# Spatial product and first output rows as half-array passes over two tiles at once, a second x group in two loads, and a newly searched order

## The chip, the cores and the metric

The kernel runs on one core of one Trainium2 chip. The core has five engines with an instruction queue each: TensorE (PE, matrix products), VectorE (DVE), ScalarE (ACT), GpSimd (POOL) and SyncE (SP, which here issues DMAs). Each queue is worked off strictly in its written order; between engines there are only semaphores. The metric is the device time of one execution in microseconds. Before the change it is 247.53 us, the median of 3 runs (247.49 to 248.48).

## The reference

Two layers on x with S = 2048 tokens and D = 448 features, all in bf16. LN is a layer norm without scale and shift.

```python
# A: windowed attention, 16 heads of 28, window of 8 keys, 2 apart, backwards
q, k, v = split(LN(x) @ wqkv)                   # wqkv 448 x 1344
attn = softmax(q . k[pos - 0, 2, ... 14] * 28 ** -0.5)
h = x + (attn @ v[same keys]) @ wo              # wo 448 x 448
# B: gated MLP with a product over tokens
z = gelu(LN(h) @ w_in)                          # w_in 448 x 1792
z1, z2 = z[:, :896], LN(z[:, 896:])
g = w_sp @ z2 + b_sp[:, None]                   # w_sp 2048 x 2048: mixes tokens
out = h + (z1 * g) @ w_out                      # w_out 896 x 448
```

Token t of g needs z2 of all 2048 tokens. So the spatial product (w_sp @ z2, the largest product of all) can begin a tile's sum with some tokens of z2, but can't end one before the last z2 tile is there.

## The kernel before, in words

Tokens are cut into 16 tiles of 128 (NB). Everything lies in SBUF; the regions of the attention stage are used again by weights and results of the gated MLP.

**Attention.** x comes in by loads of 1, 1, 2, 4, 4 and 4 tiles into `x_tm` (FIRST, `load_x`; loads have line 519 in the page, or 518 where they transpose). For each tile DVE makes the statistics (L610 BATCH_NORM_STATS2, L612 aggregate), POOL the reciprocal root for a whole group of tiles (`ln_rstd`, L604 and L605; the groups are LN1G), DVE the normalized `xn` (L621). The first four tiles are transposed on PE, the others by a transposing DMA on SP's queue (xT4 and up, into `xhT`). PE makes q and k (`qkT`), v (`V1`); small casts out of PSUM are shared between ACT and DVE (`move`, L504; the table ON says which one goes to another engine than its default). 18 blocks of queries follow: logits (L793) in small passes of 28 contraction rows, exp on ACT into `E` (L802), the mask on DVE (L808, `mk`), the product with V on PE (L817), division on DVE into `otm` (L828), a transposing DMA into `OT`, wo on PE, and the residual into x_tm on DVE (L760).

**Gated MLP.** Again statistics, root, norm, and a transposing DMA into `hnT`. Then 16 products z2_0 to z2_15 (a tile of 128 tokens, 2 x 448 columns) and 14 products z1_0 to z1_13 (2 x 512 columns, z1 transposed). ACT applies gelu; for those z2 tiles that are made while ACT still has exps to do, ACT first copies the raw sums out (z2c) and applies gelu later. DVE takes two statistics and an aggregate of each z2 tile (L877, L880), POOL makes the root for two tiles, DVE normalizes z2p in place (L886).

The spatial product has 28 tiles (fc, tc): 128 features fc by 512 tokens tc. Each is a sum over 16 token tiles s, written as four lots of 4 passes. Lot q of a tile needs the normalized z2 tiles 4q to 4q + 3:

```python
for q in range(4):
    ss = range(4 * q, 4 * q + 4)
```

A pass is one matmul instruction of the full array: 128 rows of contraction, 128 x 128 weights from `z2p`, 512 columns of `wsp_la`, `wsp_lb` or `wsp_hi`. DVE adds the bias (L957, `ub`) and multiplies into z1p (L962). After each seven tiles of one tc come four output tiles: 7 passes of 448 columns with `w_out` (L972), the residual on DVE (L979, `srg`), and the store.

**Half passes.** The contraction of a D = 448 product has three chunks of 128 and one of 64. `product()` (L461) writes the two sums of a ticket (a pair of PSUM banks) in one of three modes. FH and HF: six full passes and two half passes of 64 rows, or the other way round. AB: only half passes, two at a time. One half of the array works on the first sum with rows 0 to 63 of a chunk, the other half on the second sum with rows 64 to 127; then the halves change roles. Where one sum goes over from one half of the array to the other, the job is marked `own`, and PE waits on its own semaphore for the first half's last pass. Before the change the z products and nearly all others are in mode AB.

**The order.** Each job (a few instructions of one engine) stands in a list; a planner, run long before, has left two tables in the file: ORDER, the order in which the jobs are written into the queues, and BANKS, the PSUM banks of each ticket. Nothing is decided on the chip: an engine whose next instruction waits does no later one. `keys` and durations in the code were the planner's input, and no instruction comes out of them.

Of the kernel before, what the change touches and what calls it, by code (L numbers as in the profile page):

```python
# [6 lines left out]
D = 448  # L7
NHEAD = 16
DH = 28
FH = 896  # L10
EPS = 1e-5

NB = 16
# [16 lines left out]
ORDER = [0, 25, 27, 30, 28, 2, 938, 6, 31, 938, 938, 15, 938, 32, 938, 938, 128, 1, 938, 938, 39, 9, 26, 938, 41, 40,  # L30
# [169 lines left out]
class Ticket:  # L200
# [4 lines left out]
    def __init__(self, n):  # L205
        self.n = n
        self.b = None
        self.res = Res("ticket")


class Job:
    __slots__ = ("eng", "key", "dur", "lat", "ops", "acq", "rel", "tick",
                 "deps", "idx", "name", "tbl", "srv", "kind", "alts", "modes", "mate", "own")


class Planner:


    def __init__(self):
# [825 lines left out]
```

## Time and profile before

| | |
|---|---|
| median of 3 runs | 247.53 us |
| profiled execution | 246.68 us |
| its span | 245.0 us |
| mean granted TensorE clock | 1.000 |
| PE busy | 237.6 us (97%), 2139 instructions |
| DVE busy | 154.9 us (63%), 338 instructions |
| ACT busy | 92.6 us (38%) |
| POOL busy | 37.0 us (15%) |
| first spatial pass | 124.28 us from the span's start |
| PE's last pass ends by | 242.4 us |

The profiled execution is 1.68 us longer than its span and 0.85 us below the median. Busy shares are over the whole span: DVE's 63% is an average of a first half with nearly full slices and a second half in which it has little to do. Lines (L461) are those of the kernel before. Columns of a waits row are the total in us, the number of waits and the longest; of a group's row, busy time in us and the mean of one in ns, then the idle time ahead of them. In a timeline row stand the start, the length (for a run of several instructions, from the first's start to the last's end), the engine, the line and the instruction. PE's passes are pipelined, so lengths of single passes overlap; the step from one run's start to the next is the time that the passes took.

### The profile page before, as it was taken

The numbers are of one execution on the slowest core, as the hardware profiler recorded it, in microseconds if no ns is written. First come the engines' busy times: TensorE is split into PE (matmuls) and PEld (weight loads), VectorE is DVE, ScalarE is ACT, GpSimd is POOL, SyncE is SP. The second block draws the span as 40 slices with busy tenths as digits, with TensorE's granted clock in tenths as the row PEclk, the third lists the DMA queues.
The fourth block names the chain that finished last, engine by engine and source line by source line (L and its number), as shares of the span: only waits on it lengthen the run. The fifth ranks groups of instructions, "written<-read, shape, count | busy, mean of one in ns | idle before, by whom it ended". The sixth has DMA issues, their size and how long they took to land.

```text
span 245.0 us, 5076 instructions
## 1 busy us (share of the span) xinstructions
PE 237.6 (97%) x2139; PEld 119.9 (49%) x2139; DVE 154.9 (63%) x338; ACT 92.6 (38%) x111; POOL 37.0 (15%) x82
## 2 busy tenths in 40 slices
PE   7988999979999999999999999999999999999995
PEld 5764545444555544445444444444444444444453
DVE  5698989968997799899991120360333353271674
ACT  2379479775685979978740000000000000000000
POOL 6424020223042302323331000000000000000000
PEclk9999999999999999999999999999999999999999
DMA  5953656889969769988999400000000001001022
GB/s 144 268 171 67 89 89 118 150 182 150 219 92 162 119 94 201 238 134 119 197 195 176 98 0 0 3 0 0 0 3 0 1 19 56 3 30 45 0 65 87
DMA packets 66247, 23.16 MB, mean 95 GB/s; under 512 B 58672, under 2 KB 65968, under 8 KB 66224
## 3 DMA queue, kind: packets, MB, share of 16 engines
q1 hardware_dynamic: 66224, 22.83, 48.2%
q8 instruction: 17, 0.28, 0.5%
q14 instruction: 6, 0.05, 0.1%
HBM read 6.72 MB, written 1.84 MB: 35 GB/s over the span
## 4 chain that ended last, share of the span: by engine, by line
PE 84%; DVE 4%; DMA 4%; ACT 2%; SPq 2%; POOL 1%; issue 1%; DVEq 0%
PE psum L948 39%; PE psum L461 30%; PE psum L972 9%; PE psum L817 3%; DMA x_tm<-in_A_x_dram 2%; PE psum L793 2%; SPq L519 2%; DVE st L610 2%; DMA xhT<-xn 2%; ACT E L802 1%; DVE xn L621 1%; ACT qkT L504 1%; POOL rs L605 1%; POOL rs L604 1%; DVE x_tm L760 0%
## 5 line engine op out<-in xcount | busy, mean ns | idle before, releaser
L957 DVE TENSOR_TENSOR ub<-psum,bb 128x512 bf16<-128x512 f32 x28 | 19.4, 691 | 63.3 <-PE psum L948 62.8
L948 PE MATMUL psum<-wsp_hi,z2p 128*128 128x512 bf16 x224 | 49.2, 379 | 0.0
L948 PEld LDWEIGHTS psum<-wsp_hi,z2p 128*128 128x128 bf16 x224 | 21.9, 98 | 26.4
L802 ACT ACTIVATE E<-psum 128x896 bf16<-128x896 f32 (+2 forms) x36 | 31.9, 935 | 7.1 <-PE psum L793 7.0
L948 PE MATMUL psum<-wsp_lb,z2p 128*128 128x512 bf16 x112 | 26.0, 379 | 0.0
L948 PE MATMUL psum<-wsp_la,z2p 128*128 128x512 bf16 x112 | 25.6, 379 | 0.0
L461 PE MATMUL psum<-xhT,wqk 64*128 64x512 bf16 (+2 forms) x218 | 24.6, 350 | 0.0
L461 PE MATMUL psum<-w_in,hnT 64*128 64x448 bf16 x224 | 24.3, 349 | 0.0
L461 PE MATMUL psum<-hnT,w_in 64*128 64x512 bf16 (+1 forms) x190 | 23.7, 376 | 0.0
L972 PE MATMUL psum<-w_out,z1p 128*128 128x448 bf16 (+1 forms) x119 | 21.9, 341 | 0.0
L610 DVE BATCH_NORM_STATS2 st<-x_tm 128x6 f32<-128x448 bf16 x32 | 19.4, 611 | 2.4 <-DMA x_tm<-in_A_x_dram 2.2
L877 DVE BATCH_NORM_STATS2 st<-z2p 128x6 f32<-128x448 bf16 x32 | 19.3, 611 | 0.6 <-ACT z2p L870 0.2
L808 DVE TENSOR_TENSOR E<-E,maskb 128x1792 bf16<-128x1792 bf16 (+2 forms) x18 | 19.4, 1094 | 0.0
L605 POOL TENSOR_TENSOR rs<-rs,negh 128x2 f32<-128x2 f32 (+2 forms) x22 | 18.2, 827 | 1.8
L504 ACT ACTIVATE qkT<-psum 128x1024 bf16<-128x1024 f32 (+1 forms) x16 | 13.2, 841 | 11.2 <-PE psum L461 8.5
L948 PEld LDWEIGHTS psum<-wsp_la,z2p 128*128 128x128 bf16 x112 | 11.0, 98 | 13.1
L948 PEld LDWEIGHTS psum<-wsp_lb,z2p 128*128 128x128 bf16 x112 | 11.0, 98 | 13.1
L604 POOL TENSOR_SCALAR rs<-mv 128x2 f32<-128x2 f32 (+2 forms) x22 | 9.2, 417 | 49.7 <-DVE mv L612 30.9
L972 PEld LDWEIGHTS psum<-w_out,z1p 128*128 128x128 bf16 x119 | 11.6, 98 | 10.0
L461 PEld LDWEIGHTS psum<-w_in,hnT 64*128 64x128 bf16 x224 | 10.6, 94 | 10.5 <-ACT E L802 0.2
L461 PE MATMUL psum<-wv,xhT 64*128 64x448 bf16 x126 | 14.9, 350 | 0.5 <-DMA xhT<-xn 0.5
L915 ACT ACTIVATE z1p<-psum 128x1024 bf16<-128x1024 f32 x14 | 14.2, 1029 | 3.1 <-PE psum L461 3.0
(59 smaller groups left out, 240.1 us busy)
## 6 DMA issues: line engine op xcount, KB each, us to landing
w_in<-in_B_w_in_dram SPq DMA_DIRECT2D x8, 224.0 KB, 3.9
out_dram<-srg SPq DMA_DIRECT2D x16, 112.0 KB, 1.7
x_tm<-in_A_x_dram SPq DMA_DIRECT2D x3, 448.0 KB, 7.3
w_out<-in_B_w_out_dram SPq DMA_DIRECT2D x1, 784.0 KB, 5.3
wq<-in_A_wqkv_dram SPq DMA_DIRECT2D x3, 224.0 KB, 2.8
bb<-in_B_b_sp_dram SPq DMA_DIRECT2D x1, 512.0 KB, 4.3
wv<-in_A_wqkv_dram SPq DMA_DIRECT2D x1, 336.0 KB, 6.1
wo<-in_A_wo_dram SPq DMA_DIRECT2D x1, 336.0 KB, 6.5
```

Source lines behind the costliest of these rows:

```text
L461: ins = e.matmul(o, w, x, start=k not in seen, stop=last, **kw)
L504: j = pl.job(name, eng, key, [(lambda e: e.activation(o(), i(), AF.Copy) if eng == "act" else e.tensor_copy(o(), i()), list(reads), list(w ...
L604: [(lambda e: e.tensor_single_scalar(A, mv[:, m:m + n, 1], EPS, ALU.add), r_mv[k][m:m + n], [rr]), (lambda e: e.tensor_tensor(R, A, negh[: ...
L605: (lambda e: e.tensor_tensor(R, A, negh[:, 0:1].to_broadcast([128, n]), ALU.pow), [rr, r_negh], r_rs[k][m:m + n])],
L610: [(lambda e: e.bn_stats(st[:, m, :], src), [rsrc], [r_st[k][m]])], dve_t(D))
L802: return e.activation(o, i, AF.Exp, scale=SCALE)
L808: return e.tensor_tensor(a, a, maskb[:, 0:1, pad:pad + nq].to_broadcast([NK, NHEAD, nq]), ALU.mult)
L877: [(lambda e, m=m, k=k: e.bn_stats(st3[:, m, k, :], z2p[:, m, D * k:D * (k + 1)]), [r_z2[m]], [r_st[2][m]])], dve_t(D))
L915: return e.activation(o, i, AF.Gelu_apprx_tanh)
L948: ins = e.matmul(psv(tk), z2p[:, s, 128 * fc:128 * fc + 128], w[:, 512 * (tc % 2):512 * (tc % 2) + 512], start=(s == 0), stop=(s == NB - 1))
L957: [(lambda e, tc=tc, s=s, tk=tk: e.tensor_tensor(ub[:, s, :], psv(tk), bb[:, 512 * tc:512 * tc + 512], ALU.add), [r_bb], [r_ub[s]])], dve_ ...
L972: ins = e.matmul(psv(tk, 0, c1 - c0), z1p[:, fc, 128 * m:128 * m + 128], w_out[:, fc, c0:c1], start=(fc == 0), stop=(fc == FC7 - 1))
```

## The change: half passes in pairs, two x loads, and new tables

Four things are changed.

1. **The spatial product in pairs.** The first 26 of its 28 tiles are taken two at a time on a pair of banks (`gate_pair`). Every pass of 128 rows becomes two half passes of 64 rows: lots named a put the pair's first tile on one half of the array and the second on the other, lots named b the other way round. A pair of tiles so has 32 pairs of half passes where two tiles had 32 full passes. The first four pairs are written in eight lots, each over four token tiles (three a lots, four b lots, one a lot); the others in two lots over all sixteen, one a and one b. The last two tiles stay full passes (`gate_one`).
2. **The output rows.** Tiles 0 to 11 are taken in pairs as well (`out_pair`), with half passes except for tiles 10 and 11. Tiles 12 to 15 stay as they were.
3. **The second x group.** Tiles 4 to 7 come in two loads of two tiles, each with statistics and a root of its own.
4. **New tables.** ORDER and BANKS are new throughout, and so are some entries of MODE and of ON (which engine does a small copy or cast). DVE now does three casts of raw z2 sums (z2c3, z2c5, z2c9) that ACT did. Constants of the planner (`half_t`, the loads' costs) are changed too; no instruction depends on them.

```diff
-         'z1_5': 'AB', 'z1_6': 'AB', 'z1_7': 'AB', 'z1_8': 'AB', 'z1_9': 'AB', 'z1_10': 'HF', 'z1_11': 'AB', 'z1_12':
...
+         'v16': 'FH', 'y14': 'AB', 'z2_0': 'HF', 'z2_1': 'AB', 'z2_2': 'HF', 'z2_3': 'FH', 'z2_4': 'HF', 'z2_5': 'AB',
...
+         'AB', 'z2_14': 'AB', 'z2_15': 'AB', 'z1_0': 'FH', 'z1_1': 'FH', 'z1_2': 'AB', 'z1_3': 'AB', 'z1_4': 'FH',
...
+         'AB', 'z1_13': 'AB', 'wo0': 'AB', 'wo2': 'AB', 'wo4': 'AB', 'wo6': 'AB', 'wo8': 'AB', 'wo10': 'FF'}
-ORDER = [0, 25, 27, 30, 28, 2, 938, 6, 31, 938, 938, 15, 938, 32, 938, 938, 128, 1, 938, 938, 39, 9, 26, 938, 41, 40,
...
+ORDER = [0, 29, 130, 26, 31, 6, 28, 1, 880, 32, 880, 3, 880, 30, 880, 40, 4, 880, 27, 41, 880, 880, 42, 2, 33, 880,
...
+         'od17': 'dve', 'oc17': 'act', 'nd1_15': 'dve', 'z2c3': 'dve', 'z2c5': 'dve', 'z2c9': 'dve'}
...
-FIRST = [(0, 1), "q0", "q1", "q2", "q3", (1, 2), (2, 4), "v", (4, 8), (8, 12), (12, 16), "o"]
-LN1G = [(0, 1), (1, 1), (2, 2), (4, 4), (8, 4), (12, 4)]
+FIRST = [(0, 1), "q0", "q1", "q2", "q3", (1, 2), (2, 4), "v", (4, 6), (6, 8), (8, 12), (12, 16), "o"]
+LN1G = [(0, 1), (1, 1), (2, 2), (4, 2), (6, 2), (8, 4), (12, 4)]
...
+        def gate_pair(i):
+            pair = tiles[2 * i:2 * i + 2]
+            tk = pl.ticket(2)
+            fine = pair[0][1] == 0
+            lots = ([("a", range(4 * q, 4 * q + 4)) for q in range(3)] + [("b", range(4 * q, 4 * q + 4)) for q in range(4)]
+                    + [("a", range(12, 16))]) if fine else [("a", range(NB)), ("b", range(NB))]
+            prev = None
+            for n, (ab, ss) in enumerate(lots):
+                def f(e, ab=ab, ss=ss, n=n):
+                    for s in ss:
+                        for k, (fc, tc) in enumerate(pair):
+                            t = k if ab == "a" else 1 - k
+                            h = slice(64 * t, 64 * t + 64)
+                            ins = e.matmul(psv(tk, k), z2p[h, s, 128 * fc:128 * fc + 128], wsp(s, tc)[h], start=n == 0 and s == 0,
+                                           stop=n == len(lots) - 1 and s == ss[-1], tile_position=(64 * t, 0))
+                    return ins
...
+                if prev is not None and prev.name[-1] != ab:
+                    j.own, j.ownp = True, prev
...
+        def out_pair(m, key):
...
+                for fc in range(FC7):
+                    for k in ((0, 1) if half else (which,)):
+                        h, kw = slice(0, 128), {}
+                        if half:
+                            t = k if which == 0 else 1 - k
+                            h, kw = slice(64 * t, 64 * t + 64), {"tile_position": (64 * t, 0)}
+                        ins = e.matmul(psv(tk, k, D), z1p[h, fc, 128 * (m + k):128 * (m + k) + 128], w_out[h, fc, :],
...
+        for gi in range(2 * NP2, 28):
+            gate_one(gi)
```

What the new tables do to the queues shows at three places. In the changed kernel the lines have moved (mostly by two: L461 is L459, L877 is L875, L886 is L884; the spatial product, L948, is L964, the output rows, L972, are L1012).

SP's queue at the start, where it issues the first loads, before:

```order
L519 DMA x_tm<-in_A_x_dram 128x448
L519 DMA wq<-in_A_wqkv_dram 128x896
L519 DMA x_tm<-in_A_x_dram 128x448
L519 DMA wo<-in_A_wo_dram 64x448
L519 DMA wq<-in_A_wqkv_dram 128x896
L519 DMA wv<-in_A_wqkv_dram 64x448
L519 DMA wq<-in_A_wqkv_dram 64x448 x2
L519 DMA wq<-in_A_wqkv_dram 128x896
L519 DMA x_tm<-in_A_x_dram 128x2x448
L519 DMA x_tm<-in_A_x_dram 128x4x448
L519 DMA wv<-in_A_wqkv_dram 128x3x448
```

and now:

```order
L517 DMA x_tm<-in_A_x_dram 128x448 x2
L517 DMA wq<-in_A_wqkv_dram 128x896 x2
L517 DMA wq<-in_A_wqkv_dram 64x448
L517 DMA wq<-in_A_wqkv_dram 128x896
L517 DMA wq<-in_A_wqkv_dram 64x448
L517 DMA x_tm<-in_A_x_dram 128x2x448
L517 DMA x_tm<-in_A_x_dram 128x4x448
L517 DMA wv<-in_A_wqkv_dram 64x448
L517 DMA x_tm<-in_A_x_dram 128x2x448
L517 DMA wv<-in_A_wqkv_dram 128x3x448
L517 DMA x_tm<-in_A_x_dram 128x2x448
```

Before, the load of four tiles is that of tiles 4 to 7 (x4). Now the load of four tiles is the third group, tiles 8 to 11 (x8); x4, tiles 4 and 5, comes two rows behind it, and x6 after the large wv load. The wo load has moved behind them.

PE around the first lot of the spatial product, before:

```order
L461 MATMUL psum<-hnT,w_in 128x512 x22
L461 MATMUL psum<-w_in,hnT 128x448 x8
L461 MATMUL psum<-hnT,w_in 128x512 x6
L461 MATMUL psum<-w_in,hnT 128x448 x6
L461 MATMUL psum<-hnT,w_in 128x512 x8
L948 MATMUL psum<-wsp_la,z2p 128x512 x52
L948 MATMUL psum<-wsp_lb,z2p 128x512 x4
```

and now (448 columns are z2 products, 512 columns z1 products):

```order
L459 MATMUL psum<-w_in,hnT 128x448 x34
L964 MATMUL psum<-wsp_la,z2p 128x512 x24
L459 MATMUL psum<-w_in,hnT 128x448 x8
L459 MATMUL psum<-hnT,w_in 128x512 x8
L459 MATMUL psum<-w_in,hnT 128x448 x6
L964 MATMUL psum<-wsp_la,z2p 128x512 x8
L459 MATMUL psum<-hnT,w_in 128x512 x6
L964 MATMUL psum<-wsp_lb,z2p 128x512 x8
L459 MATMUL psum<-hnT,w_in 128x512 x8
L964 MATMUL psum<-wsp_la,z2p 128x512 x16
L964 MATMUL psum<-wsp_lb,z2p 128x512 x8
L459 MATMUL psum<-hnT,w_in 128x512 x20
```

All z products stood ahead of the first spatial pass. Now three lots of the first two pairs of tiles stand ahead of z2_15, z2_14 and z1_10 to z1_13, and the rest of these six is mixed with further lots. A pair of lots that follow each other without a matmul between them is one row here.

DVE up to the norm that makes the first lot's four z2 tiles complete, before (L877 is a statistic of z2, L886 writes normalized z2):

```order
L877 BN_STATS st_65<-z2p 128x6 x2
L880 BN_AGGR mv_66<-st_65 128x2
L877 BN_STATS st_65<-z2p 128x6
L886 TENSOR_SCALAR z2p<-z2p,mv_66,rs_69 128x896
L877 BN_STATS st_65<-z2p 128x6
L886 TENSOR_SCALAR z2p<-z2p,mv_66,rs_69 128x896 x2
```

and now:

```order
L608 BN_STATS st_63<-x_tm 128x6 x2
L610 BN_AGGR mv_64<-st_63 128x2 x2
L502 CAST z2p<-psum 128x896
L875 BN_STATS st_65<-z2p 128x6
L619 TENSOR_SCALAR xn<-x_tm,mv_64,rs_68 128x448
L875 BN_STATS st_65<-z2p 128x6
L502 COPY xn<-xn 128x64
L878 BN_AGGR mv_66<-st_65 128x2
L619 TENSOR_SCALAR xn<-x_tm,mv_64,rs_68 128x448
L875 BN_STATS st_65<-z2p 128x6 x4
L878 BN_AGGR mv_66<-st_65 128x2 x2
L884 TENSOR_SCALAR z2p<-z2p,mv_66,rs_69 128x896
```

The last norm of the first lot's tiles is the last row in both (before, one of the two in it). Now the last tiles' statistics (L608) and norms (L619) of the layer norm on h and a cast of raw z2 sums out of PSUM stand directly ahead of it on DVE; before, only work on z2 stood there.

More of the change, by code (lines that the diff above doesn't have):

```diff
@@ L212 @@
     __slots__ = ("eng", "key", "dur", "lat", "ops", "acq", "rel", "tick",
-                 "deps", "idx", "name", "tbl", "srv", "kind", "alts", "modes", "mate", "own")
+                 "deps", "idx", "name", "tbl", "srv", "kind", "alts", "modes", "mate", "own", "ownp")
 class Planner:
@@ L237, in job @@
         j.own = False
+        j.ownp = None
         deps = set(a for a in after if a is not None)
@@ new lines, in gate_pair @@
+        def gate_pair(i):
[14 more added lines that the diff above has]
+                    return ins
+                rws = [r_z2[s] for s in ss]
+                for tc in sorted({tc for _, tc in pair}):
+                    rws += [(r_whi if tc >= 2 else r_wlo)[s] for s in ss]
+                j = pl.job("g%d_%d%s" % (i, n, ab), "pe", GK + 2 * i + 0.01 * n + (2.5 if n and not fine else 0), [(f, rws, [])],
+                           512 / 2400.0 * len(ss), acq=tk if n == 0 else None, use=[tk], kind="H",
+                           after=[prev] + (z2_jobs if i >= 3 and n == 0 else []))
+                if prev is not None and prev.name[-1] != ab:
+                    j.own, j.ownp = True, prev
+                prev = j
+            for k, (fc, tc) in enumerate(pair):
+                gate_out(2 * i + k, fc, tc, tk, k, GK + 2 * i + 2.5)
@@ new lines, in gate_one, with f, out_rows @@
+        def gate_one(gi):
+            fc, tc = tiles[gi]
+            tk = pl.ticket(1)
+            def f(e):
+                for s in range(NB):
+                    ins = e.matmul(psv(tk), z2p[:, s, 128 * fc:128 * fc + 128], wsp(s, tc), start=(s == 0), stop=(s == NB - 1))
+                return ins
+            pl.job("g%d_0" % gi, "pe", GK + gi + 2.5, [(f, r_z2 + r_whi, [])], full_t(512, NB), acq=tk, use=[tk])
+            gate_out(gi, fc, tc, tk, 0, GK + gi + 2.5)
+        def out_rows(m, c0, c1, tk, k, key):
+            s = m % NS
+            pl.job("r%d" % m, "dve", key,
+                   [(lambda e: e.tensor_tensor(srg[:, s, c0:c1], psv(tk, k, c1 - c0), x_tm[:, m, c0:c1], ALU.add),
+                     [r_x[m]], r_srg[2 * s + (c0 > 0):2 * s + 1 + (c1 == D)])], dve_t(c1 - c0), use=[tk], rel=(tk, k, 1))
+            if c1 == D:
+                load("out%d" % m, lambda: OUT[128 * m:128 * m + 128, :], lambda: srg[:, s, :], [], 0.35, (0.8, 0.55),
+                     key=key, reads=r_srg[2 * s:2 * s + 2])
@@ new lines, in out_pair, with f @@
+        def out_pair(m, key):
+            tk = pl.ticket(2)
+            tc = m // 4
+            name = "wo%d" % m
+            half = MODE.get(name) == "AB"
+            def f(e, which):
+                for fc in range(FC7):
[5 more added lines that the diff above has]
+                        ins = e.matmul(psv(tk, k, D), z1p[h, fc, 128 * (m + k):128 * (m + k) + 128], w_out[h, fc, :],
+                                       start=fc == 0 and (which == 0 or not half), stop=fc == FC7 - 1 and (which == 1 or not half), **kw)
+                return ins
+            ro = [r_wout] + [r_z1[(fc, tc)] for fc in range(FC7)]
+            j1 = pl.job(name + "a", "pe", key, [(lambda e: f(e, 0), ro, [])], full_t(D, FC7), acq=tk)
+            j2 = pl.job(name + "b", "pe", key + 0.1, [(lambda e: f(e, 1), ro, [])], full_t(D, FC7), use=[tk], after=[j1])
+            for j in (j1, j2):
+                j.modes = [("FF", full_t(D, FC7), "F"), ("FF", full_t(D, FC7), "F"), ("AB", FC7 * D / 2400.0, "H")]
+            j1.mate, j2.mate = j2, j1
+            j2.own = half
+            for k in range(2):
+                out_rows(m + k, 0, D, tk, k, key + 0.5)
```

101 lines of the change are left out of this document (47 added, 54 removed), and 103 rows, old and new, of tables (BANKS, MODE, ON, ORDER).

## The prediction

> **What bounds the kernel now.** I read the page first, then the chain that ended last in order of time, then TensorE's (PE's) timeline, and then everything about VectorE (DVE) ahead of the spatial product. From the page:
>
> ```profile
> span 245.0 us, 5076 instructions
> PE 84%; DVE 4%; DMA 4%; ACT 2%; SPq 2%; POOL 1%; issue 1%; DVEq 0%
> GB/s 144 268 171 67 89 89 118 150 182 150 219 92 162 119 94 201 238 134 119 197 195 176 98 0 0 3 0 0 0 3 0 1 19 56 3 30 45 0 65 87
> ```
>
> PE carries 84% of the chain. The chain's later pieces say that from 91.75 us on PE never stops (columns: start, length, what):
>
> ```profile
> 74.02 0.90 PE psum L817 x32
> ...
> 76.73 0.50 PE psum L817 x16
> ...
> 91.75 32.69 PE psum L461 x314
> 124.44 74.25 PE psum L948 x344
> ...
> 216.07 5.30 PE psum L972 x28
> ...
> 242.38 0.39 DVE srg L979
> ```
>
> L948 is the spatial product: 74.25 us over 344 full-array passes of 512 columns is 215.8 ns each. L972 makes the output rows: 5.30 over 28 full passes of 448 columns is 189.3 ns. DVE's last eviction at 242.38 marks the end of PE's work. The products before it (L461) already run as half-array pairs, and PE's timeline gives their price:
>
> ```profile
> 106.51 3.83 PE L461 MATMUL psum<-hnT,w_in 64*128 64x512 bf16 x34
> 110.18 5.46 PE L461 MATMUL psum<-w_in,hnT 64*128 64x448 bf16 x56
> 115.48 1.03 PE L461 MATMUL psum<-hnT,w_in 64*128 64x512 bf16 x8
> 124.28 4.05 PE L948 MATMUL psum<-wsp_la,z2p 128*128 128x512 bf16 x18
> ```
>
> From one start to the next: 3.67 us for 17 pairs of 512 columns, 215.9 ns a pair; 5.30 us for 28 pairs of 448, 189.3 ns a pair. So a pair of half passes costs what a full pass costs. The first spatial pass starts at 124.28. It needs the normalized z2 tiles 0 to 3, which DVE writes (L886). DVE from the mask of attention block 1 to the last of these four:
>
> ```profile
> 11.94 0.63 DVE L610 BATCH_NORM_STATS2 st<-x_tm 128x6 f32<-128x448 bf16 x1 [1.12 <-DMA x_tm<-in_A_x_dram]
> ...
> 18.29 6.55 SPq L518 DMA_TRANSPOSE xhT<-xn  x4
> ...
> 21.65 2.19 DVE L808 TENSOR_TENSOR E<-E,maskb 128x2048 bf16<-128x2048 bf16 x2
> ...
> 122.33 0.92 DVE L886 TENSOR_SCALAR z2p<-z2p,mv,rs 128x896 bf16<-128x896 bf16 x2
> ```
>
> The masks end at 23.84, the norms at 123.24: only 1.04 us before PE asks. Between them, in a windows view (second number PE busy, fourth DVE busy) and in DVE's waits of that stretch (total, times, longest):
>
> ```profile
> 23.85:123.24 99.39, 97.40 (x1302) 49.13 (x1297) 89.41 (x203) 77.47 (x91) 22.94 (x46) 1.00 0.84 147
> ```
> ```profile
> DVE xn L621 <- POOL rs L605: 3.5, 4, 1.0
> DVE x_tm L760 <- PE psum L461: 1.4, 1, 1.4
> DVE otm L828 <- DMA OT<-otm: 1.2, 1, 1.2
> DVE qkT L504 <- PE psum L461: 0.9, 2, 0.5
> ```
>
> DVE works 89.4 of 99.4 us. Of the 10.0 us left, 7.0 are these waits and 3.0 are hand-overs and two waits of 0.2. So before the spatial product there are two full engines, PE and DVE, and DVE is done just in time.
>
> **The change part by part.** *Half passes for the spatial product and output rows.* 13 pairs of tiles become 13 x 32 = 416 pairs of half passes, 12 output tiles become 84. At 215.9 against 215.8 ns, and 189.3 against 189.3, I take a price of zero. Bounds: the slope from 448 to 512 columns is 26.6 ns for 64, so 512 columns stream in 213 ns and about 3 ns of each pass are fixed. Were that hidden, 500 pairs would give back 1.5 us. On the other side, each change of halves within a pair waits for that pair's earlier pass to end; the order always has other passes between, which cover it. Without them it would cost the tail of a pass, 0.16 us (3.83 us long, the next row starts after 3.67), at each of 22 changes: 3.5 us. The Trainium skill's page TensorEngine Tiling (Array Packing), section Key Properties, says that tiles operate independently and can load weights and multiply in parallel. Read strongly, each tile would hide the other's fixed part, and the sum would be 1.5 us lower than mine. The trace does not agree: these very pairs, in L461, show 215.9.
>
> *Mode switches.* Two groups of sixteen small passes take 0.90 us side by side and one alone 0.50, so entering another array shape costs 0.10. From the first attention output on, the order has 64 such changes where it had 59: 0.5 us, all but one ahead of the first spatial pass, where (below) PE waits for DVE anyway. Without that cover it is 0.5.
>
> *More work ahead on PE's queue.* The changed order puts the first spatial lot in front of six z products (two of 448, four of 512 columns, 7 pairs each): 14 x 0.189 + 28 x 0.216 = 8.7 us. So after the first lot PE has 118.1 us (124.28 to 242.4) + 8.7 = 126.8 us to do. To break even the four norms must end by 115.6 instead of 123.24. This is the hinge of the forecast.
>
> *DVE's queue.* The same stretch, grouped by line, before:
>
> ```profile
> L808 DVE TENSOR_TENSOR E<-E,maskb 128x1792 bf16<-128x1792 bf16 (+1 forms) x16 | 17.2, 1088 | 0.0
> L877 DVE BATCH_NORM_STATS2 st<-z2p 128x6 f32<-128x448 bf16 x27 | 16.2, 611 | 0.5 <-ACT z2p L870 0.2
> L610 DVE BATCH_NORM_STATS2 st<-x_tm 128x6 f32<-128x448 bf16 x18 | 11.0, 610 | 0.2
> L886 DVE TENSOR_SCALAR z2p<-z2p,mv,rs 128x896 bf16<-128x896 bf16 x10 | 4.8, 506 | 0.2 <-POOL rs L605 0.2
> L504 DVE CAST qkT<-psum 128x1024 bf16<-128x1024 f32 x3 | 3.7, 1221 | 0.9 <-PE psum L461 0.9
> L504 DVE COPY xn<-xn 128x64 bf16<-128x64 bf16 x16 | 2.8, 184 | 0.4
> L504 DVE COPY otm<-otm 112x64 bf16<-112x64 bf16 (+1 forms) x9 | 1.6, 176 | 0.2
> L504 DVE CAST V<-psum 128x896 bf16<-128x896 f32 x1 | 1.1, 1082 | 0.0
> L504 DVE COPY OT<-OTs 128x456 bf16<-128x456 bf16 x4 | 1.0, 249 | 0.0
> ```
>
> I count the changed order from the mask of block 1 to the norm that completes tiles 0 to 3, and price each difference by busy time over count: one mask more (+1.08), five z2 statistics fewer (-3.00), one x statistic more (+0.61), two norms fewer (-0.96), two qkT casts more and one of half the width (+2.47 + 0.62), four xn, three otm and two OT copies fewer (-0.70 - 0.53 - 0.50), one V cast more (+1.10), three new z2p casts from PSUM, as wide as V's (+3.30); the small aggregates nearly cancel. Sum +3.5: DVE has 92.9 us of work there. ACT gives these casts up, which buys nothing: it is not the engine waited for.
>
> *Start.* The second x group comes in two loads, each with its own statistics and root. SP issues one load more; its first transpose stands at 18.29 and waits for data, so this is covered. But it now puts the third group (448 KB) ahead of the second. Before, x4 landed at 11.9 with 1792 KB moved up to its end; now 1960 KB. At the page's 268 GB/s of that slice, 0.6 us more, 12.5; it cannot be used before DVE is free for it, which was at 10.8 (11.94 less 1.12 idle). I take 11.6. From its statistics to the end of block 1's mask DVE took 11.9 us (11.94 to 23.84); the new order has there two statistics, one mask, one norm and one aggregate fewer and one small copy more, -2.7, so 9.2. The mask ends at 20.8, 3 us earlier; ends 20.0 and 21.7.
>
> *Sum.* 20.8 + 92.9 + 3.0 hand-overs + waits. The waits lie between 0 and 7.0. PE- and DMA-caused ones go when PE itself is late for DVE; the 3.5 on POOL's root stay, since that chain is not touched: 3.5. The four norms end at 120.2 (ends 116 and 125), the first lot starts at 120.3, PE ends 126.8 later at 247.1, against 242.4: +4.7 us. Per item: start -3.0, DVE work +3.5, waits -3.5, earlier need +8.7, and -1.0 of slack used up. The profiled execution took 246.68 us, 1.7 more than its span; this gives 251.4. The median of the runs shown is 247.53, 0.85 higher, so 252.2 by it; I forecast 251.6.
>
> Little follows behind: the norms of tiles 8 to 11 lie 6 us of DVE work further on (6 statistics x 0.60, 4 norms x 0.48, 3 aggregates), and the order gives PE 6.3 us of passes before it wants them; the evictions of the spatial product have room (DVE waited 62.8 us for them, next row); the rows after the last tile are as before.
>
> **The rivals.**
>
> ```profile
> DVE ub L957 <- PE psum L948: 62.8, 12, 14.3
> PE psum L461 <- ACT qkT L504: 1.5, 1, 1.5
> ```
>
> *PE stays dense (faster).* If DVE never holds PE up, PE meets its first spatial lot at 124.28 - 8.7, less 1.5 us of the wait above, less some 2 for the earlier start: 112.1, and ends at 238.9, 243.2 us for the execution. The mechanism is an earlier start carried to the end; it decides at 115.6 us for the four norms. For it: DVE idled 10.0 us in that stretch, and an order that feeds it better could use them. Against it: even with no wait at all, 20.8 + 92.9 + 3.0 is 116.7. It needs the start at its early end and some hand-overs gone as well. 0.14, mostly near 245.
>
> *DVE waits for nothing.* Norms at 116.7, PE's end at 243.6: 247.9, just within half a per cent. 0.15.
>
> *Half passes hide the fixed part.* Likeliest case less 1.5: 249.9. It changes no sign; 0.1 of the slower cases.
>
> *x4 lands later still.* If it waits for the whole third group and the wv load behind it, 13 us or more, every microsecond goes to the end: 253 and up. 0.1.
>
> *The change does not do what it says.* If two half passes ran one after the other, 416 pairs would add 90 us; the L461 rows exclude it.
>
> **How the numbers follow.** Half a per cent, 1.2 us, is about what a measurement of this kernel can tell from no change. Chances: DVE holds PE up by more than that 0.71 (the likeliest, with the two variants above); nearly in time 0.15; PE dense 0.14. So faster 0.14, same 0.15, slower 0.71. The likeliest case's own range, from the waits' ends (3.5 either way) and the start's (0.6 and 0.9), is 247.5 to 256. The whole range starts at 246.8, which leaves out most of the faster case, and ends at 256.
>
> **What would show it.** Right: PE waits, some 8 us in all between about 65 and 120 us, for DVE's norms and for what hangs on them (hnT transposes, banks that DVE still reads), the last just before the first pass of wsp_la; DVE with 92 to 94 us of work and few idle gaps from its first mask on; 215.8 ns per pair in the spatial product; about 126.8 us from its first pass to PE's end; x4 landing between 11 and 12.5. Wrong: the first lot starting by 115 us, a pair at 213 ns or over 217, gaps inside the spatial product, or a start that is not earlier.

## The result

The changed kernel takes 244.09 us (median of 4 runs, 243.74 to 245.33), the kernel before 248.00 beside it. The ratio is 0.985 (95% interval 0.980 to 0.990): 1.5% faster, where 1.6% slower was forecast. Its profiled execution took 243.96 us with a span of 242.2. Run again (e0_after) it took 244.29 us against 247.60, a ratio of 0.988 (0.981 to 0.995). Medians are of all executions, while a ratio leaves out those that took over 1.5% longer than the fastest of the same kernel, so it can differ a little from the quotient of the medians.

The page and the chain in order of time, after:

```profile
span 242.2 us, 5928 instructions
PE 80%; DMA 7%; ACT 5%; DVE 5%; SPq 2%; issue 0%; DVEq 0%
```
```profile
98.27 14.62 PE psum L459 x146
112.90 2.59 PE psum L964 x24
...
131.95 31.08 PE psum L964 x288
193.30 2.65 PE psum L1012 x28
...
239.63 0.39 DVE srg L993
```

PE runs without a stop from 98.27 us to the end. A pair of half passes costs 31.08 / 144 = 215.8 ns, the price of the full pass before it; 14 pairs of the output rows cost 2.65 us, 189.3 ns each. The first spatial pass starts at 112.72 (next fence), the last output pass ends by 239.6: 126.9 us for what is left, where the prediction had 126.8. So in this execution all that the forecast missed lies ahead of the first spatial pass. There, DVE from the end of its first mask to the norm that completes z2 tiles 0 to 3 (timeline and windows, columns as before):

```profile
19.06 1.08 DVE L806 TENSOR_TENSOR E<-E,maskb 128x1792 bf16<-128x1792 bf16 x1
...
111.58 0.46 DVE L884 TENSOR_SCALAR z2p<-z2p,mv,rs 128x896 bf16<-128x896 bf16 x1
```
```profile
112.72 2.77 PE L964 MATMUL psum<-wsp_la,z2p 64*128 64x512 bf16 x24
```
```profile
20.15:112.10 91.95, 91.16 (x1200) 47.46 (x1196) 87.94 (x195) 69.29 (x82) 23.62 (x51) 1.00 0.71 139
```
```profile
DVE rcp L823 <- PE psum L815: 0.9, 3, 0.5
DVE qkT L502 <- PE psum L459: 0.8, 1, 0.8
DVE z2p L884 <- POOL rs L603: 0.4, 2, 0.3
DVE xn L619 <- POOL rs L603: 0.4, 1, 0.4
```

The mask ends at 20.14, the norms at 112.04, 0.7 us before PE takes them. The forecast was 20.8 and 120.2. DVE is busy for 87.9 of 92.0 us, with 4.0 us idle; 92.9 and 6.5 were forecast. Waits for POOL's root, of which 3.5 us were to stay, are 0.8 in all.

### The profile page after: what moved, and what is told of

The parts are those of the page before. It is cut to its first block, busy times and chain, and to the rows that moved or that the text cites. A ratio compares the mean times of both kernels' runs of the same rounds, so it can differ in the third digit from the quotient of the medians.

```text
span 242.2 us, 5928 instructions
## 1 busy us (share of the span) xinstructions
PE 236.7 (98%) x2568; PEld 128.2 (53%) x2568; DVE 149.7 (62%) x336; ACT 89.8 (37%) x107; POOL 37.7 (16%) x90
## 4 chain that ended last, share of the span: by engine, by line
PE 80%; DMA 7%; ACT 5%; DVE 5%; SPq 2%; issue 0%; DVEq 0%
PE psum L964 37%; PE psum L459 26%; PE psum L1012 7%; ACT E L800 3%; PE psum L985 3%; DMA hnT<-xn 3%; PE psum L1033 2%; PE psum L791 2%; DMA x_tm<-in_A_x_dram 2%; PE psum L815 2%; DMA OTs<-otm 2%; SPq L517 2%; DVE st L875 1%; ACT V L502 1%; DVE z2p L502 1%; PE psum L692 1%
## 5 line engine op out<-in xcount | busy, mean ns | idle before, releaser
L964 PE MATMUL psum<-wsp_hi,z2p 64*128 64x512 bf16 x384 | 43.2, 376 | 0.0
L964 PEld LDWEIGHTS psum<-wsp_hi,z2p 64*128 64x128 bf16 x384 | 21.7, 94 | 19.4
L875 DVE BATCH_NORM_STATS2 st<-z2p 128x6 f32<-128x448 bf16 x32 | 19.1, 614 | 12.8 <-ACT z2p L871 12.2
L964 PE MATMUL psum<-wsp_lb,z2p 64*128 64x512 bf16 x224 | 26.5, 376 | 0.0
L964 PE MATMUL psum<-wsp_la,z2p 64*128 64x512 bf16 x224 | 26.5, 376 | 0.0
L459 PE MATMUL psum<-w_in,hnT 64*128 64x448 bf16 (+1 forms) x200 | 25.4, 350 | 0.5 <-ACT E L800 0.3
L459 PE MATMUL psum<-hnT,w_in 64*128 64x512 bf16 (+1 forms) x178 | 24.7, 377 | 0.0
L459 PE MATMUL psum<-xhT,wqk 64*128 64x512 bf16 (+2 forms) x218 | 23.8, 349 | 0.2
L608 DVE BATCH_NORM_STATS2 st<-x_tm 128x6 f32<-128x448 bf16 x32 | 18.8, 612 | 2.3 <-DMA x_tm<-in_A_x_dram 2.2
L964 PEld LDWEIGHTS psum<-wsp_lb,z2p 64*128 64x128 bf16 x224 | 12.7, 94 | 11.4
L964 PEld LDWEIGHTS psum<-wsp_la,z2p 64*128 64x128 bf16 x224 | 12.7, 94 | 11.3
L1012 PE MATMUL psum<-w_out,z1p 64*128 64x448 bf16 (+1 forms) x154 | 17.4, 349 | 0.0
L459 PEld LDWEIGHTS psum<-w_in,hnT 64*128 64x128 bf16 (+1 forms) x200 | 11.3, 94 | 11.5 <-issue 1.5
L459 PEld LDWEIGHTS psum<-xhT,wqk 64*128 64x128 bf16 (+1 forms) x218 | 10.5, 94 | 9.7 <-ACT E L800 0.5
L459 PEld LDWEIGHTS psum<-hnT,w_in 64*128 64x128 bf16 (+1 forms) x178 | 10.2, 94 | 9.9 <-ACT z2p L868 0.4
L459 PE MATMUL psum<-wv,xhT 64*128 64x448 bf16 (+1 forms) x114 | 14.6, 351 | 0.0
## 6 DMA issues: line engine op xcount, KB each, us to landing
out_dram<-srg SPq DMA_DIRECT2D x16, 112.0 KB, 1.7
```

The source lines that it names most:

```text
L459: ins = e.matmul(o, w, x, start=k not in seen, stop=last, **kw)
L608: [(lambda e: e.bn_stats(st[:, m, :], src), [rsrc], [r_st[k][m]])], dve_t(D))
L875: [(lambda e, m=m, k=k: e.bn_stats(st3[:, m, k, :], z2p[:, m, D * k:D * (k + 1)]), [r_z2[m]], [r_st[2][m]])], dve_t(D))
L964: ins = e.matmul(psv(tk, k), z2p[h, s, 128 * fc:128 * fc + 128], wsp(s, tc)[h], start=n == 0 and s == 0, stop=n == len(lots) - 1 and s == ...
L1012: ins = e.matmul(psv(tk, k, D), z1p[h, fc, 128 * (m + k):128 * (m + k) + 128], w_out[h, fc, :], start=fc == 0 and (which == 0 or not half) ...
```

## The experiments

Runs with the same "before" were timed beside the same executions of the kernel before. "Span" is that of the profiled execution; "first lot" is the start of the first spatial pass. In every variant of the changed kernel in which the passes behind it are the changed kernel's, 126.6 us pass from there to the start of the last pass.

| run | median us | before | ratio (95%) | span | first lot |
|---|---|---|---|---|---|
| changed kernel, first | 244.09 | 248.00 | 0.985 (0.980 to 0.990) | 242.2 | 112.7 |
| e0_after | 244.29 | 247.60 | 0.988 (0.981 to 0.995) | 241.5 | 112.0 |
| e1_full_late | 244.80 | 247.54 | 0.991 (0.987 to 0.994) | 243.7 | 113.9 |
| e2_full_all | 246.17 | 247.54 | 0.997 (0.993 to 1.000) | 245.2 | 114.3 |
| e5_adjacent | 249.38 | 247.54 | 1.011 (1.004 to 1.018) | 247.6 | 118.1 |
| e9_oT3 | 246.33 | 247.54 | 0.997 (0.994 to 1.000) | 244.7 | 124.0 |
| e4_load_order | 251.70 | 247.60 | 1.017 (1.010 to 1.023) | 249.6 | |
| e8_spread | 252.03 | 247.60 | 1.017 (1.011 to 1.024) | 250.4 | |
| e10_both | 251.96 | 247.60 | 1.018 (1.012 to 1.023) | 250.2 | |
| e3_one_load | 245.08 | 247.58 | 0.993 (0.989 to 0.996) | 243.4 | 113.9 |
| e6_casts_act | 244.10 | 247.58 | 0.989 (0.985 to 0.993) | 242.8 | 113.3 |
| e7_six_more | 245.96 | 247.58 | 0.995 (0.991 to 0.998) | 244.1 | 114.6 |
| e11_wo_later | 246.96 | 247.58 | 1.001 (0.997 to 1.005) | 244.0 | 123.4 |
| e12_before | 247.65 | 247.69 | 1.001 (0.998 to 1.004) | 245.6 | 124.9 |
| e13_two_moves | 245.50 | 247.69 | 0.991 (0.989 to 0.994) | 243.4 | 122.7 |
| e14_ve12 | 244.60 | 247.69 | 0.987 (0.984 to 0.990) | 242.1 | 112.6 |
| e4b_x8_last | 248.94 | 247.69 | 1.006 (1.003 to 1.009) | 246.7 | |

### What the half passes are worth: e1_full_late, e2_full_all

```diff
+        FULL = 4
...
                 def f(e, ab=ab, ss=ss, n=n):
+                    if i >= FULL:
+                        k = 0 if ab == "a" else 1
+                        fc, tc = pair[k]
+                        for s in ss:
+                            ins = e.matmul(psv(tk, k), z2p[:, s, 128 * fc:128 * fc + 128], wsp(s, tc), start=s == 0, stop=s == NB - 1)
+                        return ins
                     for s in ss:
...
-         'AB', 'z1_13': 'AB', 'wo0': 'AB', 'wo2': 'AB', 'wo4': 'AB', 'wo6': 'AB', 'wo8': 'AB', 'wo10': 'FF'}
+         'AB', 'z1_13': 'AB', 'wo0': 'FF', 'wo2': 'FF', 'wo4': 'FF', 'wo6': 'FF', 'wo8': 'FF', 'wo10': 'FF'}
```

FULL is 4 in the first and 0 in the second.

> The changed kernel with the same order, but the spatial pairs 4 to 12 and the output rows 0 to 9 as full passes. Theory A (a pair of half passes costs what a full pass costs, and the gain lies elsewhere): span 242.0 to 242.6 us against 242.2 of the changed kernel, and 215.8 ns for a full pass as for a pair. Rival B (half passes hide each other's fixed part, and that is the gain): 243.3 to 245 us.

> As before it, with the first four pairs as full passes too, so that no spatial or output pass is a half pass. These lots are mixed with the last z products, which stay half passes: some 15 more changes of the array's shape at 0.093 us each. Theory A: 1.4 us more than the run with only the late pairs changed, span 243.4 to 244.0. If the changes of shape are hidden: 242.0 to 242.6. Rival B: 245 or more.

e1's span came out at 243.7, inside the range written for rival B, but not by B's mechanism: PE was already 1.2 us late at its first spatial pass, before any edited instruction (in that execution it waited 1.2 us at 23.6 us, where the changed kernel had no such wait). From there to the start of the last pass it took 126.8 us against 126.6, and its order has 3 changes of the array's shape behind that point instead of 1. The full passes cost as much as the pairs. e1's median is 0.5 to 0.7 us above the changed kernel's two; 0.2 of that lies behind the first spatial pass, the rest was not separated. Chains of e1 and then of the changed kernel:

```profile
170.68 24.17 PE psum L965 x112
```
```profile
169.13 24.17 PE psum L964 x224
```

e2 took 128.0 us from its first lot, 1.4 more than the changed kernel, and its median is 1.4 above e1's. Its PE timeline shows what a change of the array's shape costs, about 0.1 us (117.04 less 114.34 is 2.70 us for 12 passes of 215.8 ns, which make 2.59):

```profile
114.34 2.76 PE L965 MATMUL psum<-wsp_la,z2p 128*128 128x512 bf16 x12
117.04 0.93 PE L459 MATMUL psum<-w_in,hnT 64*128 64x448 bf16 x8
```

So theory A holds: the half passes bring nothing by streaming. What they do is let spatial lots stand between z products without 14 more changes of shape (15 in e2, 1 in the changed kernel), 1.4 us in all.

### VectorE's neighbours: e5_adjacent, e8_spread

DVE's timeline before (first fence) and after (second). Before, an instruction that waits for the one directly ahead of it, nearly always because it reads what that one has written, starts 0.03 us after that one's recorded end (46.17 + 0.63 = 46.80, then 46.83); one that does not starts 0.08 us ahead of the end (46.83 + 0.18 = 47.01, then 46.93). After, readers and writers hardly ever stand next to each other.

```profile
46.17 0.63 DVE L610 BATCH_NORM_STATS2 st<-x_tm 128x6 f32<-128x448 bf16 x1
46.83 0.18 DVE L612 BATCH_NORM_AGGREGATE mv<-st 128x2 f32<-128x6 f32 x1
46.93 0.59 DVE L610 BATCH_NORM_STATS2 st<-x_tm 128x6 f32<-128x448 bf16 x1
```
```profile
107.35 0.62 DVE L875 BATCH_NORM_STATS2 st<-z2p 128x6 f32<-128x448 bf16 x1
107.88 0.38 DVE L619 TENSOR_SCALAR xn<-x_tm,mv,rs 128x448 bf16<-128x448 bf16 x1
108.18 0.62 DVE L875 BATCH_NORM_STATS2 st<-z2p 128x6 f32<-128x448 bf16 x1
```

Between the first mask and the norms of tiles 0 to 3 the kernel before has 64 such neighbours, the changed one 5. The run e5 puts 63 of them there again, by moving writers down. (ORDER itself is a table of numbers; here and below such a cut gives a stretch of one queue by the names of its jobs, before and after the edit.)

```diff
 # VectorE's queue by job, behind h8: h residual, n norm, nd its copy, st statistic, mv aggregate
-h8, n1_7, st1_9, rc16, nd1_7, mv1_9, n1_6
+h8, n1_7, nd1_7, st1_9, mv1_9, n1_6
```

> The changed kernel with VectorE's statistics, reciprocals and norms moved down until each stands directly ahead of the aggregate, division or copy that reads it, as in the kernel before: 63 such neighbours between the first mask and the norms of z2 tiles 0 to 3 where there were 5. In the traces a reader starts 0.117 us later than an independent instruction would: 58 x 0.117 = 6.8 us of VectorE. Theory C (VectorE is just in time, and its order is what made room for the change): span 245 to 248 us, the first spatial pass 3 us or more later than 112.7. Rival D (VectorE has room to spare): 242.0 to 242.6.

The time went to 249.38 us, 5.1 more than the second run of the changed kernel (4.6 more than e1, timed beside it) and 1.1% slower than the kernel before. The stretch holds the same instructions and now takes 96.7 us where it took 92.0. Of these 4.7 us, 4.6 are DVE's busy time (92.55 against 87.94), and its idle time is 4.1 us against 4.0: the neighbours themselves are the cost, not new waits of DVE. With a mask that ends 1.2 us later the norms end 6.0 us later, at 118.03, and PE waits for DVE on the way, in eight rows of its waits, of which three stand here:

```profile
21.36:118.03 96.67, 92.47 (x1192) 46.09 (x1192) 92.55 (x197) 69.56 (x81) 23.22 (x51) 1.00 0.70 132
```
```profile
PE psum L789 <- DVE qkT L500: 1.1, 2, 0.6
PE psum L457 <- DVE x_tm L756: 1.0, 1, 1.0
...
PE psum L962 <- DVE z2p L882: 0.2, 1, 0.2
```

Theory C holds for the changed kernel: span and first lot are within what it had written down, while the price of 6.8 us for the neighbours came out at 4.7. The reverse, taking neighbours apart in the kernel before, is no cure by itself:

```diff
 # VectorE's queue by job: mk mask, rc reciprocal, om division, od its copy, qe cast of q and k
-mk4, qe4_1, mk5, rc3, om3, od3, rc4, om4, od4, mk6, rc5, om5, h0
+mk4, mk5, rc3, qe4_1, om3, rc4, od3, om4, mk6, rc5, od4, h0, om5
```

> The kernel before with VectorE's order alone changed: neighbours of which the second reads the first's result are taken apart by exchanging them with the next independent instruction, 64 between the mask of block 1 and the norms of z2 tiles 0 to 3, now none (7 us of VectorE by the 0.117 us each). Theory C (room on VectorE is needed for a gain but is none by itself, PE waits 1 to 2 us in all for VectorE there): 0.5 to 1.5 us less than the kernel before. Rival H (VectorE sets the whole first half): 2.5 us less or more. Rival D: no change.

> The kernel before with VectorE's order as in the run ahead and the transposing DMA of attention block 3 issued ahead of that of block 4. The DMA's move alone gave 1.35 us at 54 us and kept 0.2 at the end, PE then waited for VectorE. Theory C: with room on VectorE the 1.35 us pass to the end, 1.5 to 2.8 us less than the kernel before, without one half pass in the spatial product. Rival B (the gain needs half passes): at most 0.5 us less.

Both took 252.0 us; none of the theories had forecast a loss. In e8, DVE is busy for 87.7 of the 108.5 us from 23.5 us on, where before it was for 89.4 of 99.4: the neighbours' cost is gone, and idle time has taken its place. The exchanges put a mask or a residual ahead of a cast or a division that PE or SP was waiting for; PE waits 1.4 us for a qkT cast alone, DVE 7.4 us for POOL's root, and after that wait of PE, at 40 to 42 us, the clock falls (windows of e8, PE's columns, then the granted clock):

```profile
40.00:42.00 2.00, 0.57 (x27) 1.00 0.41 30
...
43.00:44.00 1.00, 1.00 (x20) 0.54 0.83 190
44.00:45.00 1.00, 1.00 (x8) 0.50 0.44 97
45.00:46.00 1.00, 1.00 (x8) 0.50 1.10 218
46.00:47.00 1.00, 1.00 (x10) 0.75 0.99 204
47.00:48.00 1.00, 1.00 (x18) 1.00 0.88 204
```

So it seems that what goes between two dependent instructions must itself be due there; no run tests this by itself.

### VectorE's load: e7_six_more, e6_casts_act, e14_ve12

```diff
                          [r_st[2][m]])]
+                       + [(lambda e, m=m, k=k: e.bn_stats(dum[:, 2 * m + k, :], z2p[:, m, D * k:D * (k + 1)]), [r_z2[m]], [])
+                          for _ in range(m in (1, 2, 4))], dve_t(D))
```

> The changed kernel with six statistics of z2 done twice (tiles 1, 2 and 4, into a tile that nobody reads): 6 x 0.53 = 3.2 us more for VectorE between 82 and 95 us. Theory C (VectorE is just in time, 0.7 us ahead of PE at the first spatial pass, with 1.3 us of idle time behind 82): 1.2 to 2.5 us more than the changed kernel. Rival D (room to spare): within 0.3 us.

245.96 us, 1.7 more than the second run of the changed kernel; the first lot starts 1.9 us later than in the changed kernel's first profile. DVE has little room, as theory C says. In e6 ScalarE does the three casts of raw z2 sums again; e14 besides gives one cast of values to DVE:

```diff
-         'od17': 'dve', 'oc17': 'act', 'nd1_15': 'dve', 'z2c3': 'dve', 'z2c5': 'dve', 'z2c9': 'dve'}
+         'od17': 'dve', 'oc17': 'act', 'nd1_15': 'dve'}
 # e14 besides
-         'dve', 've4': 'dve', 'nd1_3': 'dve',
+         'dve', 've4': 'dve', 've12': 'dve', 'nd1_3': 'dve',
```

> The changed kernel with the three casts of raw z2 sums on ScalarE again, at the same places of the order: VectorE has 3.2 us less to do between 81 and 107 us, ScalarE 2.5 us more. The forecast said that this hand-over buys nothing, since ScalarE is not waited for: then the kernel takes as long as the changed one or up to 0.5 us less. Rival I (ScalarE is the engine that PE waits for there): 0.8 to 2.5 us more.

> The changed kernel with the three casts of raw z2 sums on ScalarE, and one cast of values (blocks 12 and 13, at 61 us on ScalarE) on VectorE, which waits 0.5 us there. PE's waits between 64 and 71 us, 1.1 us behind ScalarE's exps, shrink by up to 0.8 us: 0.2 to 0.8 us less than the changed kernel. Rival: VectorE hands the 1.1 us on, 0.3 to 0.8 us more.

Both are as fast as the changed kernel (244.10 and 244.60 against 244.09 and 244.29). The hand-over of casts buys nothing, as the forecast said, but it costs nothing either: with 3.2 us less on DVE, the first lot starts no earlier (113.3 us): behind the start, PE in e6 waits nowhere for VectorE; it waits 0.6 us for ScalarE and 0.6 for a transpose into hnT. e14 did not gain what was hoped: PE's waits for ScalarE are 1.0 us in its profile, and 0.3 and 0.8 in the two of the changed kernel.

### The start: e3_one_load, e4_load_order, e4b_x8_last

```diff
-FIRST = [(0, 1), "q0", "q1", "q2", "q3", (1, 2), (2, 4), "v", (4, 6), (6, 8), (8, 12), (12, 16), "o"]
+FIRST = [(0, 1), "q0", "q1", "q2", "q3", (1, 2), (2, 4), "v", (4, 8), (8, 12), (12, 16), "o"]
```

> The changed kernel with tiles 4 to 7 in one load again, at the place of the first of the two; their two roots and everything else stay. Theory G (the start passes to the end): the statistics of tiles 5 and 4 wait for 224 KB more, about 0.8 to 1.3 us, and the kernel takes 0.5 to 1.3 us more than the changed one. Rival J (VectorE has other tiles' statistics to do meanwhile): within 0.3 us.

245.08 us, 0.8 to 1.0 more than the changed kernel's two runs (and 1.0 more than e6, timed beside it); PE is 0.7 us behind the changed kernel's first profile at 16 us and 1.2 at the end. The two loads are a part of the gain.

```diff
 # e4, SyncE's first loads
-x0, x1, wq0, wq2, wq3, wq1, wq4, x2, x8, wv_1, x4, wv, x6, wv_0, wo_0, wo, wo_1, x12
+x0, wq1, x1, wo_0, wq0, wv_0, wq3, wq4, wq2, x2, x4, x6, wv, wo, x12, wo_1, x8, wv_1
 # e4b, against the same first line
+x0, x1, wq0, wq2, wq3, wq1, wq4, x2, x4, x6, wv_1, wv, x8, wv_0, wo_0, wo, wo_1, x12
```

> The changed kernel with the first loads issued in the order of the kernel before (wo, wv and wq pieces between the x tiles, x8 behind x12), the two loads of tiles 4 to 7 next to each other. Theory G (the earlier start, 1.6 us more product work done at 16 us, comes from this order and passes to the end): 1.2 to 2 us more than the changed kernel. Rival: PE's later waits absorb it, under 0.5 us more.

> The changed kernel with the four-tile load x8 issued behind x4, x6 and wv instead of ahead of x4. Data of tiles 4 to 7 come up to 1.5 us earlier, those of 8 to 11 later; VectorE's order takes a statistic of tile 9 first. Theory (VectorE's order at the start is bound to the loads' order): 0.3 to 1.5 us more than the changed kernel. Rival (an earlier x4 is all that counts): 0.3 to 1 us less.

Much worse than any theory had it: 251.70 and 248.94 us. A part is the granted clock, whose mean is 0.993 or 0.986 in all four executions of e4 and in six of the seven of e4b; a fall is priced below at 1.4 us. Both keep DVE's written order, which takes a statistic of tile 9 (x8) ahead of tiles 5 and 4. In e4b it holds up everything behind it:

```profile
13.19 0.63 DVE L606 BATCH_NORM_STATS2 st<-x_tm 128x6 f32<-128x448 bf16 x1 [3.40 <-DMA x_tm<-in_A_x_dram]
```

These two show that the orders of loads and of DVE belong together, not what the load order alone is worth. That is better seen in the kernel before:

### SyncE's queue in the kernel before: e9_oT3, e11_wo_later, e13_two_moves, e12_before

```diff
 # e9: SyncE's transposes of attention blocks (oT) and loads
-w_in1_1, oT4, w_in1_0, oT5, oT3, wlo1
+w_in1_1, oT3, oT4, w_in1_0, oT5, wlo1
 # e11: SyncE's first loads
-x0, wq1, x1, wo_0, wq0, wv_0, wq3, wq4, wq2, x2, x4, wv
+x0, wq1, x1, wq0, wq3, wq4, wq2, x2, x4, wo_0, wv_0, wv
```

e13 is both. PE's longest wait in the kernel before, and SP around it:

```profile
52.41 0.93 PE L461 MATMUL psum<-wo,OT 64*128 64x448 bf16 x8 [1.46 <-ACT qkT L504]
```
```profile
45.19 1.21 SPq L518 DMA_TRANSPOSE OT<-otm  x1
46.45 0.58 SPq L519 DMA_DIRECT2D w_in<-in_B_w_in_dram  x1
47.12 2.98 SPq L518 DMA_TRANSPOSE OT<-otm  x2
```

The row names ScalarE, but that cast had ended at 51.67. What ended at 52.3 is the DMA of block 3, the second of the pair at 47.12, whose OT the product reads.

> The kernel before with one move on SyncE's queue: the transposing DMA of attention block 3 is issued ahead of that of block 4 and not four places later. PE's longest wait, 1.5 us at 50.9, ends with its landing at 52.3, although the waits row names ScalarE. Theory E (that wait is part of the gain, and it passes to the end): span 243.4 to 244.2 us against 245.0. Rival F (VectorE's order keeps the first spatial pass at 124.3): 244.7 to 245.2.

> The kernel before with two small loads on SyncE's queue moved: one piece of wo and one of wv, fourth and sixth, are issued behind x4, as the changed kernel has it. The q and k weights and x2, x4 are then issued 0.5 to 1.2 us earlier. Theory G: PE is 0.5 to 1.2 us ahead at 16 us and 0.3 to 1.2 us less is measured at the end. Rival F (the kernel before is held by VectorE's order further on): under 0.3 us at the end.

> The kernel before once more. Theory K (PE's wait of 1.5 us near 51 us lets the clock fall to half for some 3.4 us, as after a wait of that length in the run with VectorE's neighbours taken apart): where its mean clock is 0.993, the time is 1.5 to 1.7 us longer, and the profile shows granted clock 0.5 just behind 51 us. Rival L (the clock falls at the start, or anywhere): 0.5 elsewhere.

> The kernel before with two moves on SyncE's queue and nothing else: the pieces of wo and wv behind x4, and block 3's transposing DMA ahead of block 4's. Theory K: mean clock 1.000 in nearly every run; the start's lead of 1.0 us stays. Span 243.6 to 244.2, median 245.0 to 245.8 us against 247.6. Rival B (only the new order with its half passes gives a gain): 246.5 or more.

e9: the wait is gone and PE is 1.7 us ahead of the first profile at 54 us (0.4 of it from before the moved DMA); at 70 us 0.2 is left, and most of the rest went to waits for DVE (0.8 us at 54, 0.4 at 61), so rival F was right about the profile. Yet the median is 1.2 us lower. The reason is the clock. The kernel before, profiled again in e12, shows it (first fence) where the first profile had 1.00 throughout (second):

```profile
50.00:52.00 2.00, 0.48 (x12) 0.27 (x12) 0.73 (x4) 1.82 (x3) 0.00 (x0) 1.00 0.34 71
52.00:54.00 2.00, 2.00 (x34) 1.13 (x32) 1.90 (x6) 0.23 (x1) 0.24 (x1) 0.74 0.93 210
54.00:56.00 2.00, 2.00 (x12) 0.75 (x10) 1.27 (x2) 0.70 (x1) 0.00 (x0) 0.50 2.00 218
56.00:58.00 2.00, 2.00 (x20) 0.92 (x18) 1.93 (x8) 0.00 (x0) 0.18 (x1) 0.91 0.47 65
```
```profile
54.00:56.00 2.00, 2.00 (x26) 0.99 (x22) 1.93 (x5) 0.93 (x1) 0.00 (x0) 1.00 1.36 221
```

Right behind the wait the clock is at half. Over 90 executions of the kernel before, the mean clock is 1.000 in 15 (median 246.2 us), 0.993 in 60 (247.6) and 0.986 in 14 (249.2); one has 0.999. So one fall costs about 1.4 us, and most executions have one; 0.986 would be two, and no profile shows where the second lies. Without the wait, in e9, all 10 executions have 0.999 or 1.000, and their 246.33 us is what the kernel before takes without a fall. All 8 executions of the changed kernel have 0.999 or 1.000 too. Theory K holds, with a price a little under its 1.5 to 1.7 us.

e11 shows a lead over the first profile of 0.9 us at 20 us that is still 0.9 at the end. Part of it is chance (the second profile of the kernel before was 0.7 us ahead of the first at 20 us too), so its times decide. Over all its executions the ratio of 1.001 (0.997 to 1.005) does not tell it from no change. It keeps the wait and the fall (0.993 or less in 8 of 10 executions). At clock 1.000 it took 245.68 (2 executions) against 246.2, at 0.993 246.96 against 247.6: 0.5 to 0.6 us less. e13 keeps the lead and loses the fall: 245.50 us, clock 1.000 in all 6, which is 0.8 less than e9 at the same clock. Two moves of three small DMAs on SP's queue so give 2.2 us of some 3.4, with no half pass in the spatial product. No version was faster than the changed kernel by more than the runs can tell.

## Why the prediction was wrong

- **Price of a half pass: right.** 215.8 ns a pair was forecast by L461's rows and measured. The strong reading of the Trainium skill's page TensorEngine Tiling (Array Packing), section Key Properties, by which tiles hide each other's fixed part, is not borne out: the chains of e1 and of the changed kernel need 24.17 us for the same work in full passes and in pairs.
- **Work behind the first lot: right.** 126.8 forecast, 126.9 measured. Changes of shape: 0.10 us each (1.4 us for 14), as priced; that half passes save 14 of them where lots and z products are mixed was not said.
- **Start: nearly right.** The mask ends at 20.14 (20.8, with 20.0 to 21.7 as ends). That two loads matter is shown by e3; in the kernel before, small loads that no longer stand ahead of the weights were worth some 0.5 to 0.8 us (e11, e13).
- **DVE's queue and its sum: this step failed.** "20.8 + 92.9 + 3.0 hand-overs + waits" gave 120.2 for the norms; they ended at 112.04, and the first lot at 112.7 lies ahead of the 115 us that the prediction itself had named as a sign of being wrong. The list of instructions was right: what it adds and removes is in the trace. But it took the busy time before as a fixed amount, added differences at busy over count, and kept hand-overs and POOL waits. Added up over DVE's groups of instructions, busy time is 98.0 us before and 99.8 after, +1.8 and not +3.5. Of these sums 8.6 us before and 11.9 after are time in which one group's instruction overlaps the next one's, more of it now since a reader seldom follows its writer; idle time went from 10.0 to 4.0 us, where 6.5 was kept. So 1.7 + 3.3 + 2.5 us, and 0.7 from the start, make the 8.2 us. "That chain is not touched" was wrong of POOL's root in the same way: its instructions are the same, but other work now stands between aggregate and norm. e5 is the test: with the neighbours of before, 4.6 us more of busy time in the same list of instructions, 5.1 us in the end, and the kernel is slower than before. The page VectorE: DVE Perf Modes of the Trainium skill, section The DRAIN you can't avoid, has it that a chain of copies takes as long with a semaphore after each as with one at the end, and its table under Rules for kernel authors says to save operations and not semaphores. It does not say whether one copy waited for the one ahead of it. Here the 0.03 us behind and the 0.08 us ahead differ by 0.11 us for each neighbour that waits; the measurement decides.
- **The rival that came true** is the one of a dense PE, at 0.14: first lot 112.1 (measured 112.7), execution 243.2 us (243.96). It was held down by "even with no wait at all, 20.8 + 92.9 + 3.0 is 116.7", which is the same wrong sum.
- **From the profiled execution to the median: a second step that failed.** The 0.85 us between 246.68 and 247.53 were carried along as a constant. They are the clock: the profiled execution was one of the few without a fall (these have a median of 246.2 us), and the changed kernel has none; behind its start, the longest PE wait in its first profile is 0.3 us. This is some 1.4 of the 3.4 us gained, and the windows at 1.00 could not show it; the wait of 1.5 us could. The Trainium skill's page TensorE: Matmul & The Clock Gate, Part 1, says that the clock falls to half after an idle window of about 3.4 us that runs freely, and that it is variable from run to run. The runs agree on half and on the variability. The windows of e12 lose (0.26 + 0.50 + 0.09) x 2 = 1.7 us of clock, as half of 3.4 us would; the medians differ by 1.4. But here 1.5 us of waiting among short passes was enough, in about five executions of six.

How the 3.4 us add up is shown in parts: 1.4 from the clock (e9, e12), 0.5 to 0.8 from the first loads (e11; e13 against 246.2 at clock 1.000 and against e9), 0.8 to 1.0 from the two x loads (e3). The 0.2 to 0.7 left are the rest of the new order; it was not separated. That the parts add up is assumed: the first two were measured in the kernel before, the third in the changed one. What e5 and e2 take away is no further part of this sum: the order of DVE and the half passes are what the new order needs to come out at this time at all. Whether the order could have been had without half passes is answered by e2 for this order: 246.17, most of the gain gone.

## What to carry to other kernels

Price an in-order engine's stretch by neighbours, not by busy time: on DVE an instruction that reads its neighbour's result started 0.11 us later, and 5 of them where there were 64 made the room that this change needed (with 63, in e5, the same stretch took 4.7 us more); but fill the gap only with work that is due. Where the median is above the profiled execution, look at each execution's mean granted clock before carrying the difference over, and look for the PE wait that goes before a fall: here a wait of 1.5 us was followed, in about five executions of six, by a fall that cost 1.4 us more. And check what a wait's row names against when that work ended: here it was the order of a DMA queue.

## What was not expected of the hardware

In the kernel before, with its PE wait of 1.5 us, the mean clock shows a fall in 74 of 90 executions; where it was profiled, the fall lay right behind that wait. The other executions had none. The length of the wait alone does not decide it: e4b's profiled execution has a PE wait of 3.1 us at 11.4 us and a clock of 1.00 throughout, while six other executions of e4b show a fall. The profiles of e1, e2 and e7 have waits of 1.2 to 1.3 us, and none of their 30 executions shows a fall.
